# Moving 30 of 2048 score units of an attention kernel from the exponential of ScalarE to a polynomial on VectorE

## The chip, the cores and the metric

The kernel runs on one core of a Trainium2 chip. A core has TensorE (PE, matrix products into PSUM), ScalarE (ACT, functions such as exp), VectorE (DVE, elementwise work), GpSimd (POOL) and SyncE (SP, which here only issues transfers). The engines run their own instruction queues in order and meet through semaphores. The metric is the time of one execution on the device, in microseconds (us); lower is better. Matrix products have a weight load (PEld) ahead of them, which the profile lists for itself.

## What is computed

```python
def reference(A_x, A_wqkv, A_wo, B_x, B_wqkv, B_wo, gate_w):
    x = A_x                                             # (1, 2048, 640), bf16
    g = sigmoid((x * gate_w).sum(-1, keepdims=True))
    a = A_ref(x, A_wqkv, A_wo)    # full attention: 32 heads of 20, softmax over all 2048 keys
    b = B_ref(x, B_wqkv, B_wo)    # local attention: 32 heads of 20, 8 keys at distances 0, 2, ..., 14 back
    return g * a + (1 - g) * b
```

Both branches project x to queries, keys and values with a 640 x 1920 matrix, scale the scores by 20 ** -0.5, and project the result with a 640 x 640 matrix. `B_x` is not used. The exponentials of the full branch are by far the largest piece: 32 heads x 2048 x 2048 of them.

## The kernel before

**Score units.** The full branch is cut into 4 blocks of 512 queries (`qc`), 8 quads of 4 heads (`q`), 16 blocks of 128 keys (`kb`) and 4 heads in a quad (`j`). One (qc, q, kb, j) is a *unit*: a matmul of 128 keys by 512 queries (`mk_qk`, L1107), an exponential from PSUM to an SBUF buffer in bf16 (`mk_exp`, L1122), and a matmul of that with the values (`mk_pv`, L1130), which adds 21 rows (20 values and the sum) to one PSUM bank, `OB`. There are 2048 units. A (qc, q) is a *head group* of 64 units; there are 32, numbered `gi`.

**Steps.** Units are taken in order, alternately three and two at a time (`ST`), in the banks 0 to 2 and 3 to 4. One such set is a step, and one instruction of ScalarE does its exponentials. There are 819 steps. The scores of step s + 2 are issued after the exponential of step s. Value matmuls come in batches, some steps later; six buffers (`ebuf`) hold the exponentials until then.

**Lanes.** All other work is put between the steps by a planner that runs while the program is written. It keeps a model clock for each engine, with a cost for each instruction. Each piece of side work is a Python generator, a *lane*, with a first and a last step (`_Lane`). A lane yields before each piece, and `ready` lets it go on when the model finds room on TensorE (`lim_pe`) or VectorE (`lim_dve`) in the present step. Lanes whose name begins with a letter of `EAGER` have precedence. Others are paced by their window: they are due when they have spent less than their share. `force` writes out a lane without regard to room, where something needs its result at once. The banks 6 and 7 are shared by all lanes through `take` and `give`.

The lanes are: keys, queries and values of the full branch (`gen_k`, `gen_q`, `gen_v`, mostly in head groups 0 to 7, but queries in every group); `gen_norm` for each finished group, which transposes `OB` (`do_norm`, L630), divides by the sums (L638 to L644) and transposes back into a slot of `oTn` (L647), with the scratch tile `rg`; and, for each of the four query blocks `tc`, the local branch: `gen_F` (queries and keys of the local branch, L796, the products of L827 and sums over heads, to eight score rows), `gen_K` (values, L859, the softmax of L877 to L893, and the weighted sum on VectorE, L935 to L951), and `gen_fold` (output projection of both branches together, L677, with one output transfer for each 128 rows). For the last query block `gen_prefold` does most of the fold early (L698, L699), and `last_fold` the rest after the loop.

**Order of the local branch.** `FWIN`, `KWIN` and `OWIN` (L1258 to L1260) give the windows of the lanes F, K and O (fold) for each query block, in head groups; `gstep` turns head groups into steps. K waits for the F of its block; the last addition for each 128 rows of a K, L951, waits until the fold of the block before is through (L948), since both use `oBacc`. `oTn` has `NOT` slots, so that the normalisation of group `NOT` writes the slot of group 0, and the fold of its query block must be done by then (L1365 to L1368).

**Filler.** Where a step leaves TensorE without enough work, `idle_mm` (L1246, L1250) writes matmuls on dead data.

Of the kernel before, what the change touches and what calls it, by code (L numbers as in the profile page):

```python
# [5 lines left out]
FP32 = mybir.dt.float32  # L6
# [18 lines left out]
PADB = (WIN - 1) * DIL  # L25
SCALE = float(DH) ** -0.5
VW = 22


class _Task:  # L30
# [202 lines left out]
def _build(ctx, nc, A_x, A_wqkv, A_wo, B_wqkv, B_wo, gate_w, out):  # L233
# [49 lines left out]
    rg = [sb([P, 512], FP32, "rg")] * 2  # L283
    rr = [sb([P, 16], FP32, "rr%d" % i) for i in range(2)]
    rgn = [sb([P, 16, 32], BF16, "rgn")] * 2
    NOT = 16
    oTn = sb([P, NOT, 512], BF16, "oTn")
    itmp = oTn[:, 13, 0:256].bitcast(I32)
    stmp = oTn[:, 14, 0:320].bitcast(I32).rearrange("p (c k) -> p c k", c=CN)
    stmpf = oTn[:, 15, 0:320].bitcast(FP32).rearrange("p (c k) -> p c k", c=CN)  # L290
    zg = sb([P, KBN], FP32, "zg")
    gA = sb([P, 4 * KBN], FP32, "gA")
    gB = sb([P, KBN], FP32, "gB")
# [123 lines left out]
    free_at = {6: 0.0, 7: 0.0}  # L417
    forcing = [0]
    cur = [None]
    EAGER = "kqv"  # L420

    wanting = set()

# [17 lines left out]
    def give(b, evac):  # L441
        held[b] = False
        if cur[0] is not None:
            cur[0].hold -= 1
        free_at[b] = evac.fin + 56.0

    def after(t):
        return ("t", t.fin + 56.0)
# [96 lines left out]
    def gen_q(gi):  # L545
        qc, q = divmod(gi, NQUAD)
        i = gi % 2
        yield ("dve", 370.0, 0.0)
        yield after(mk_wq(q, i))
        while ("KM", q) not in sch.bufs:  # L550
            yield ("poll",)
        b = yield from take()
        t = yield from chain(b, proj_mms(b, WqP[i], qc), [("WqP", i), "xT"])
        yield ("dw", t.fin, 690.0, 0.0)
        t = q_abs(b, gi)
        while ("KM", q) not in sch.bufs:
            yield ("poll",)
        yield ("t", max(t.fin, sch.bufs[("KM", q)][0].fin))
        yield ("pe", MM, 1.0)
        t = q_km(b, q)  # L560
        yield ("dw", t.fin, 690.0, 0.0)
        give(b, q_cp(b, gi))
# [86 lines left out]

    bdone = {}  # L650
    folddone = {}
    FW = D // 2

    def b_mm(o, blk, c0, dp):
# [11 lines left out]
    def gen_fold(qc):  # L666
        while not bdone.get(qc) or not all(normdone.get(qc * NQUAD + q) for q in range(NQUAD)):
            yield ("poll",)
        for blk in range(4):
            for hf in range(2):  # L670
                c0 = FW * hf
                b = yield from take()
                o = bank[b][:, 0:FW]
                mms = [b_mm(o, blk, c0, dp) for dp in range(CN)] + [a_mm(o, qc, q, blk, c0) for q in range(NQUAD)]
                t = yield from chain(b, mms, b_rd(blk) + a_rd(qc, range(NQUAD)), cost=140.0)
                yield ("dw", t.fin, 490.0, 0.0)
                give(b, T("dve", lambda e, b=b, blk=blk, c0=c0: e.tensor_copy(outsb[:, c0:c0 + FW], bank[b][:, 0:FW]),  # L677
                          reads=[("bk", b)], writes=["outsb"], cost=460))
            T("sp", lambda e, blk=blk: e.dma_start(out_v[:, 4 * qc + blk, :], outsb[:, :]),
              reads=["outsb"], writes=[("outd", qc, blk)], dma=True)  # L680
        folddone[qc] = True

    NPF = NQUAD - 2
# [162 lines left out]
    def gen_K(tc):  # L846
# [80 lines left out]
        for bl in range(4):  # L927
            ai = bl % 2
            for w in range(WIN):
                av = fap(bw, attnT[ai][:, w * P:w * P + 1], [[0, CN], [1, P]])  # L930
                off = PADB - DIL * w + bl * P
                vv = vB4[:, :, off:off + P]
                yield ("dve", 822.0, 822.0)
                if w == 0:
                    T("dve", lambda e, vv=vv, av=av: e.tensor_tensor(blkacc[:, :, :], vv, av, ALU.mult),  # L935
                      reads=[("aT", ai), "vB4"], writes=["blkacc"], cost=822)
                    if bl < 3:
                        yield ("dve", 460.0, 460.0)
                        tr = mk_rep(bl + 1)
                    continue  # L940
                T("dve", lambda e, vv=vv, av=av: e.tensor_tensor(tmpB, vv, av, ALU.mult),  # L941
                  reads=[("aT", ai), "vB4"], writes=["tmpB"], cost=822)
                yield ("dve", 822.0, 822.0)
                if w < WIN - 1:
                    T("dve", lambda e: e.tensor_tensor(blkacc[:, :, :], blkacc[:, :, :], tmpB, ALU.add),  # L945
                      reads=["tmpB"], writes=["blkacc"], cost=822)
                else:
                    while tc >= 1 and not folddone.get(tc - 1):  # L948
                        yield ("poll",)
                    acc = oBacc[:, :, bl * P:(bl + 1) * P]  # L950
                    T("dve", lambda e, acc=acc: e.tensor_tensor(acc, blkacc[:, :, :], tmpB, ALU.add),  # L951
                      reads=["tmpB", "blkacc"], writes=[("oBacc", bl)], cost=822)
                if w == 3 and bl < 3:
                    yield after(tr)
                    b = yield from take()
                    yield ("pe", 550.0, 300.0)
                    tm = mk_aT(bl + 1, b)
                if w == 4 and bl < 3:
                    yield ("dw", tm.fin, 690.0, 690.0)
                    give(b, ev_aT(bl + 1, b))  # L960
        bdone[tc] = True


    mk_wk(0)
# [120 lines left out]
    free_at[6] = free_at[7] = t_  # L1085


    units = [(qc, q, kb, j) for qc in range(QCN) for q in range(NQUAD) for kb in range(KBN) for j in range(4)]
    steps = []
    u = 0  # L1090
    while u < len(units):
# [27 lines left out]
    def mk_exp(s):  # L1119
        b0 = ST[s % 2][0]  # L1120
        n = len(steps[s])
        return T("act", lambda e: e.activation(ebuf[s % NEB][:, 0:512 * n], ps[:, b0 * 512:(b0 + n) * 512], ACTF.Exp, scale=SCALE),  # L1122
                 reads=[("bk", b0 + i) for i in range(n)], writes=[("ebuf", s % NEB)], cost=ED[n])

    def mk_pv(s, us, cost):

        def fn(e):
            ins = None
            for i, (qc, q, kb, j) in us:
                ins = e.matmul(bank[OB][32 * j:32 * j + DH + 1, :], vA[:, q, kb, VW * j:VW * j + DH + 1],  # L1130
                               ebuf[s % NEB][:, i * 512:(i + 1) * 512], start=(kb == 0), stop=(kb == KBN - 1))
            return ins

        rd = {("ebuf", s % NEB)}
        wr, ac = [], []
        for i, (qc, q, kb, j) in us:
            rd.add(("vA", q, kb // 3))
            (wr if kb == 0 else ac).append(("ob", j))
        T("pe", fn, reads=sorted(rd, key=str), writes=wr, accum=ac, cost=cost)

    lanes = []
# [5 lines left out]
    def lane(gen, name, s0, s1, total, pos=None):  # L1147
        g = _Lane(gen, name, s0, s1, total)
        if pos is None:
            lanes.append(g)  # L1150
        else:
            lanes.insert(pos, g)
        return g
# [75 lines left out]

    def gstep(g):  # L1230

        return int(g * KBN * 4 / 2.5)

    def idle_mm():

# [16 lines left out]
              reads=["zt", "ident"], accum=[("ob", j) for j in range(4)], cost=MM)  # L1252
        return True

    kl, vl, ql, foldl = {}, {}, {}, {}
    vl[0] = lane(gen_v(0, 2), "v0", 0, 22, 10)
    lane(gen_late(), "late", 22, gstep(3), 1)
    FWIN = ((3.0, 8.6), (8.6, 13.2), (13.3, 18.3), (18.4, 23.5))  # L1258
    KWIN = ((8.7, 13.0), (13.2, 18.3), (18.4, 23.5), (23.6, 29.2))
    OWIN = ((13.0, 16.5), (18.4, 23.0), (23.6, 28.5))  # L1260
    FTOT, KTOT, OTOT = 58.0, 25 * 250.0 + 5 * 690 + 5 * 300 + 690 + 1880 * 2 + 1215 + 950 + 1500 + 4 * (460 + 690 + 15 * 822), 104.0
    for tc in range(4):
        lane(gen_F(tc), "F%d" % tc, gstep(FWIN[tc][0]), gstep(FWIN[tc][1]), FTOT)
    for tc in range(4):
        lane(gen_K(tc), "K%d" % tc, gstep(KWIN[tc][0]), gstep(KWIN[tc][1]), KTOT)
        if tc < 3:
            foldl[tc] = lane(gen_fold(tc), "O%d" % tc, gstep(OWIN[tc][0]), gstep(OWIN[tc][1]), OTOT)
    pre = lane(gen_prefold(3), "pre", gstep(30) + 4, NS - 3, 88.0)

    def lead(q):  # L1270
# [14 lines left out]
    for s in range(NS):  # L1285
# [4 lines left out]
        if first:  # L1290
            ng = gi + 1
            if ng < QCN * NQUAD:
                nqc, nq_ = divmod(ng, NQUAD)
                g_end = gstep(gi + 1)
                if nqc == 0:
                    if nq_ % 2 == 1 and nq_ < NQUAD - 1:
                        p = (nq_ + 1) // 2
                        vl[p] = lane(gen_v(p), "v%d" % p, s + (20 if s == 0 else 2), gstep(gi + 2) + 8, 16.0)
                    ql[ng] = lane(gen_q(ng), "q%d" % ng, s + 4, g_end - 8 - lead(ng), 6.0, 2 if s == 0 else 1)
                else:  # L1300
                    ql[ng] = lane(gen_q(ng), "q%d" % ng, s + 2, g_end - 10, 6.0, 0)
        E = mk_exp(s)
        odd = s % 2 == 1
        block[0], block[1] = False, 0.0
# [66 lines left out]
                        lane(gen_norm(g1), "norm%d" % g1, s, s + 1, 1.0, 0)  # L1371

        if gend:
            flush(False, True)
        npend = s - pend[0][0] + 1 if pend else 0
        if (odd and npend >= 3) or s >= NS - 2:
# [92 lines left out]
```

## Time and profile before

| what | value |
|---|---|
| median of 3 runs | 962.57 us (961.73 to 962.77) |
| the profiled execution | 961.62 us |
| its span | 959.8 us |
| granted TensorE clock | 0.999 |
| instructions | 16367 |
| matmuls of L1107, L1130, L1246 | 2068, 2048, 316 |
| DMA | 12.86 MB, mean 13 GB/s |

The span runs from the first to the last instruction. Rows of groups read: line, engine, operation, output<-input with shapes, number; then busy time in us and the mean of one in ns; then idle time of the engine just before them. The rows of digits are the busy share in tenths in 40 equal slices of 24 us. Pieces of a chain read: start in us, length in us, what. The first exponential of the loop starts at 19.3 us, the last at 950.5 us.

### The profile page before, as it was taken

What the parts mean: (1) busy time and instruction counts of PE and PEld (TensorE: products, weight loads), DVE (VectorE), ACT (ScalarE), POOL (GpSimd) and SP (SyncE); (2) the same over time, 40 slices, a digit from 0 to 9 for tenths busy, and PEclk for the clock granted to TensorE, in tenths of its full rate; (3) what the DMA queues carried; (4) which work ended last, traced back from release to release, by engine and by line L of the source; (5) the groups of instructions that cost most, each with busy time, mean ns of one, the idle gap of its engine ahead of it and who ended that gap; (6) DMA issues with size and microseconds to landing.
All of it is one profiled execution on the core that took longest, in us unless ns stands there. A gap on an engine that the chain in (4) does not pass through costs nothing.

```text
span 959.8 us, 16367 instructions
## 1 busy us (share of the span) xinstructions
PE 860.9 (90%) x6317; PEld 288.6 (30%) x6418; DVE 572.2 (60%) x1054; ACT 943.2 (98%) x845; POOL 3.1 (0%) x7
## 2 busy tenths in 40 slices
PE   8999898998898888889988889999989998998887
PEld 5333333322222222223322222333222233222232
DVE  5585443445424888762457798355888635897232
ACT  5999999999999999999999999999999999999997
POOL 1000000000000000000000000000000000000000
PEclk9999999999999999999999999999999999999999
DMA  9000000000000000000000000000000000000000
GB/s 312 5 1 22 15 1 1 1 25 12 1 1 1 1 1 1 2 1 8 15 8 1 1 1 1 8 8 8 9 1 1 1 9 14 9 1 1 1 1 29
DMA packets 12032, 12.86 MB, mean 13 GB/s; under 512 B 3380, under 2 KB 11316, under 8 KB 11956
## 3 DMA queue, kind: packets, MB, share of 16 engines
q1 hardware_dynamic: 9844, 11.43, 3.7%
q8 instruction: 53, 0.87, 0.4%
q10 hardware_dynamic: 2112, 0.37, 0.2%
q14 instruction: 23, 0.19, 0.1%
HBM read 9.18 MB, written 2.62 MB: 12 GB/s over the span
## 4 chain that ended last, share of the span: by engine, by line
ACT 73%; issue 17%; PE 8%; DMA 1%; DVE 1%; SPq 0%; ACTq 0%
ACT ebuf L1122 73%; PE ps L1107 3%; PE ps L1246 2%; PE ps L387 1%; PE ps L1130 1%; DMA x_tm<-in_A_x_dram 1%; ACT L_sb L884 0%; PE ps L980 0%; PE ps L719 0%; DVE Kmax L1011 0%; PE ps L811 0%; PE ps L576 0%; PE ps L911 0%; DVE oTn L738 0%; SPq L325 0%
## 5 line engine op out<-in xcount | busy, mean ns | idle before, releaser
L1122 ACT ACTIVATE ebuf<-ps 128x1536 bf16<-128x1536 f32 (+1 forms) x819 | 929.0, 1372 | 1.0
L1107 PE MATMUL ps<-qT,kT 32*128 32x512 bf16 x2068 | 321.9, 382 | 67.0 <-ACT ebuf L1122 54.7
L1107 PEld LDWEIGHTS ps<-qT,kT 32*128 32x128 bf16 x2068 | 89.0, 91 | 347.1 <-issue 145.1
L1130 PE MATMUL ps<-ebuf,vA 128*21 128x512 bf16 x2048 | 172.0, 382 | 0.0
L1246 PE MATMUL ps<-xT,ident 128*128 128x512 bf16 x316 | 122.7, 389 | 16.1 <-PE ps L1107 6.3
L941 DVE TENSOR_TENSOR bw<-vB,bw 128x640 f32<-128x640 bf16 x112 | 91.8, 820 | 2.1
L945 DVE TENSOR_TENSOR blkacc<-blkacc,bw 128x640 f32<-128x640 f32 x96 | 79.0, 823 | 2.9
L827 DVE TENSOR_TENSOR prod<-qk 128x512 bf16<-128x512 bf16 x160 | 57.4, 418 | 20.0 <-PE ps L811 19.8
L630 DVE STREAM_TRANSPOSE rg<-ps 128x512 f32<-128x512 f32 x31 | 22.2, 717 | 78.1 <-PE ps L1130 78.1
L1130 PEld LDWEIGHTS ps<-ebuf,vA 128*21 128x21 bf16 x2048 | 42.0, 90 | 72.2 <-issue 50.4
L1246 PEld LDWEIGHTS ps<-xT,ident 128*128 128x128 bf16 x358 | 34.3, 96 | 97.1 <-PE ps L1246 58.7
L387 PE MATMUL ps<-xT,WqkB 128*128 128x512 bf16 x179 | 58.2, 384 | 2.2 <-PE ps L1107 1.4
L796 DVE CAST qk<-ps 128x512 bf16<-128x512 f32 x40 | 27.5, 687 | 48.0 <-PE ps L387 46.0
L387 PE MATMUL ps<-woA_r,oTn 128*128 128x320 bf16 x240 | 50.4, 302 | 0.1
L387 PE MATMUL ps<-xT,WqP 128*128 128x512 bf16 (+1 forms) x154 | 43.3, 375 | 1.5 <-issue 0.6
L566 DVE CAST qT<-ps 128x512 bf16<-128x512 f32 x31 | 21.4, 690 | 38.4 <-PE ps L387 38.4
L387 PE MATMUL ps<-xT,WkP 128*128 128x512 bf16 (+1 forms) x151 | 42.6, 375 | 1.9 <-issue 1.1
L399 DVE TENSOR_SCALAR kT<-ps,e 128x512 bf16<-128x512 f32 x28 | 21.0, 749 | 36.8 <-PE ps L387 36.6
L583 DVE CAST qT<-ps 128x512 bf16<-128x512 f32 x31 | 21.4, 689 | 22.3 <-PE ps L576 22.1
L387 PE MATMUL ps<-WvA,oBacc 128*128 128x320 bf16 x160 | 33.1, 301 | 0.5 <-PE ps L1107 0.4
L859 DVE CAST vB<-ps 128x512 bf16<-128x512 f32 x20 | 13.7, 686 | 26.9 <-PE ps L387 26.9
L470 PE MATMUL ps<-WvA,xT 128*128 128x160 bf16 (+1 forms) x320 | 29.5, 233 | 0.0
(109 smaller groups left out, 484.2 us busy)
## 6 DMA issues: line engine op xcount, KB each, us to landing
x_tm<-in_A_x_dram SPq DMA_DIRECT2D x3, 640.0 KB
out_dram<-outsb SPq DMA_DIRECT2D x12, 160.0 KB
WqkB<-in_B_wqkv_dram SPq DMA_DIRECT2D x1, 1600.0 KB
WqkA<-in_A_wqkv_dram SPq DMA_DIRECT2D x2, 700.0 KB
qk<-in_B_wqkv_dram SPq DMA_DIRECT2D x1, 800.0 KB
woA_r<-in_A_wo_dram SPq DMA_DIRECT2D x32, 25.0 KB
WvA<-in_B_wo_dram SPq DMA_DIRECT2D x5, 160.0 KB
x_tm<-in_A_x_dram SPq DMA_DIRECT2D x2, 320.0 KB
```

The costliest lines, as they stand in the source:

```text
L387: ins = e.matmul(o, l, r, start=(k0 + k == 0), stop=(k0 + k == n - 1))
L470: ins = e.matmul(bank[b][:, i_ * wn:(i_ + 1) * wn], xT[:, c, kb * P:(kb + 1) * P], WvA[:, c, w0:w0 + wn], start=(c == 0), stop=(c == CN - 1))
L566: T("dve", lambda e: e.tensor_copy(qt[:, :], bank[b]), reads=[("bk", b)], writes=[("qT", gi % NQT)], cost=690)
L630: return T("dve", lambda e: e.transpose(rg[i][:, :], bank[OB]), reads=[("ob", j) for j in range(4)], writes=["rg"], cost=720)
L796: give(b, T("dve", lambda e, dst=dst, b=b: e.tensor_copy(dst, bank[b]), reads=[("bk", b)], writes=[key], cost=690))
L827: t = T("dve", lambda e, r=r, f=f, off=off: e.tensor_tensor(prod[r][:, :], qB[:, f, :], kB[:, f, off:off + 512], ALU.mult), reads=["qB", " ...
L941: T("dve", lambda e, vv=vv, av=av: e.tensor_tensor(tmpB, vv, av, ALU.mult), reads=[("aT", ai), "vB4"], writes=["tmpB"], cost=822)
L945: T("dve", lambda e: e.tensor_tensor(blkacc[:, :, :], blkacc[:, :, :], tmpB, ALU.add), reads=["tmpB"], writes=["blkacc"], cost=822)
L1107: ins = e.matmul(bank[b0 + i], kT[32 * j:32 * j + 32, q, kb * P:(kb + 1) * P], qT[gi % NQT][32 * j:32 * j + 32, :], start=True, stop=True)
L1122: return T("act", lambda e: e.activation(ebuf[s % NEB][:, 0:512 * n], ps[:, b0 * 512:(b0 + n) * 512], ACTF.Exp, scale=SCALE), reads=[("bk" ...
L1130: ins = e.matmul(bank[OB][32 * j:32 * j + DH + 1, :], vA[:, q, kb, VW * j:VW * j + DH + 1], ebuf[s % NEB][:, i * 512:(i + 1) * 512], start ...
L1246: T("pe", lambda e: e.matmul(bank[b], ident[:, :], xT[:, 0, 0:512], start=True, stop=True), reads=["xT", "ident"], writes=[("bk", b)], cos ...
```

## The change

For 30 of the 2048 units the exponential is taken from ScalarE. `XN` says how many units of each of the 32 head groups (0, 1 or 2), `XPOS` which. They are left out of `units`, so the steps are made of the 2018 that remain. Each of the 30 becomes a lane of its own, `gen_x`, with precedence (`EAGER` gets an x), in a window inside its head group. It takes bank 6 or 7, makes the scores there, and computes the exponential with eight instructions of VectorE in fp32: a multiply-add that puts the score, times log2 e, into the exponent field of a floating-point number; the split into exponent and mantissa by bit masks; and a polynomial of the mantissa. Then a value matmul of its own adds to `OB`. What is not done when the group ends is forced ahead of the group's last value matmuls. Two fp32 buffers `xb` are added; `rg` is used as a third, between two normalisations.

The local branch gets other windows, its lanes are listed in another order (K, then folds, then F), and the last addition of a K now waits for the fold of its own 128 rows rather than for the whole fold. `oTn` has 14 slots instead of 16, and `gstep` counts the uneven groups.

```diff
+XC4 = 0.013534167746750096
+XA = (-0.5785127719334512, 30.316837144955663, -17.76242689806009, 576.1803657752102)
+XMUL = SCALE * 1.4426950408889634 * 2.0 ** 23
+XADD = (127.0 + np.log2(XC4)) * 2.0 ** 23
+XN = (0, 0, 1, 1, 1, 2, 2, 0, 1, 0, 0, 0, 0, 1, 2, 0, 0, 1, 1, 1, 1, 1, 0, 1, 2, 2, 1, 2, 1, 2, 1, 2)
+FWIN = ((3.1, 4.4), (7.0, 11.7), (14.3, 18.8), (21.1, 25.7))
+KWIN = ((6.3, 11.3), (6.0, 16.6), (15.3, 22.4), (24.3, 29.9))
+OWIN = ((8.5, 12.7), (15.5, 20.2), (21.7, 25.8))
+XPOS = ((7, 1), (9, 2), (5, 0))
...
-    NOT = 16
+    NOT = 14
+    xb = [sb([P, 512], FP32, "xb%d" % i) for i in range(2)]
...
-    EAGER = "kqv"
+    EAGER = "kqvx"
...
+            foldblk[(qc, blk)] = True
...
-                    while tc >= 1 and not folddone.get(tc - 1):
+                    while tc >= 1 and not foldblk.get((tc - 1, bl)):
...
+    def gen_x(gi, k, u):
+        qc, q, kb, j = u
+        while k > 0 and not xdone.get((gi, k - 1)):
+            yield ("poll",)
+        while gi > 0 and not normdone.get(gi - 1):
+            yield ("poll",)
+        A, B, C = xA[:, :], xB[:, :], xC[:, :]
+        kA, kB_, kC = "xA", "xB", "rg"
+        b = yield from take()
+        yield ("pe", MM, 0.0)
+        t = T("pe", lambda e: e.matmul(bank[b], kT[32 * j:32 * j + 32, q, kb * P:(kb + 1) * P], qT[gi % NQT][32 * j:32 * j + 32, :],
+                                       start=True, stop=True),
+              reads=[("kT", q, kb // 4), ("qT", gi % NQT)], writes=[("bk", b)], cost=MM)
+        yield ("dw", t.fin, 690.0, 690.0)
+        give(b, T("dve", lambda e: e.tensor_scalar(A, bank[b], float(XMUL), float(XADD), op0=ALU.mult, op1=ALU.add),
+                  reads=[("bk", b)], writes=[kA], cost=690))
+        Ai, Bi = A.bitcast(I32), B.bitcast(I32)
+        ops = [
+            (430.0, lambda e: e.tensor_scalar(Ai, A, float(2 ** 23), None, op0=ALU.max), [kA], [kA]),
+            (430.0, lambda e: e.tensor_scalar(Bi, Ai, 0x7FFFFF, 0x3F800000, op0=ALU.bitwise_and, op1=ALU.bitwise_or), [kA], [kB_]),
+            (690.0, lambda e: e.scalar_tensor_tensor(C, B, XA[0], B, ALU.add, ALU.mult), [kB_], [kC]),
+            (430.0, lambda e: e.tensor_scalar(Ai, Ai, 0x7F800000, None, op0=ALU.bitwise_and), [kA], [kA]),
+            (690.0, lambda e: e.scalar_tensor_tensor(B, C, XA[2], B, ALU.add, ALU.add), [kC, kB_], [kB_]),
+            (690.0, lambda e: e.scalar_tensor_tensor(C, C, XA[1], B, ALU.add, ALU.mult), [kB_, kC], [kC]),
+            (690.0, lambda e: e.scalar_tensor_tensor(xe, C, XA[3], A, ALU.add, ALU.mult), [kA, kC], [kB_]),
+        ]
+        for c, fn, rd, w in ops:
+            yield ("dve", c, c)
+            t = T("dve", fn, reads=rd, writes=w, cost=c)
+        while (gi, j) not in obstart or (q, kb // 3) not in vdone:
+            yield ("poll",)
+        yield after(t)
+        yield ("pe", MM, 0.0)
+        T("pe", lambda e: e.matmul(bank[OB][32 * j:32 * j + DH + 1, :], vA[:, q, kb, VW * j:VW * j + DH + 1], xe, start=False,
+                                   stop=False, skip_group_check=True),
+          reads=[kB_, ("vA", q, kb // 3)], accum=[("ob", j)], cost=MM)
+        xdone[(gi, k)] = True
...
-    FWIN = ((3.0, 8.6), (8.6, 13.2), (13.3, 18.3), (18.4, 23.5))
-    KWIN = ((8.7, 13.0), (13.2, 18.3), (18.4, 23.5), (23.6, 29.2))
-    OWIN = ((13.0, 16.5), (18.4, 23.0), (23.6, 28.5))
...
+            n = len(xunits[gi])
+            for k in range(n):
+                sa, sb_ = s + 6, gstep(gi + 1) - 6
+                xl[(gi, k)] = lane(gen_x(gi, k, xunits[gi][k]), "x%d.%d" % (gi, k), sa + k * (sb_ - sa) // n,
+                                   sa + (k + 1) * (sb_ - sa) // n, 4740.0, 0)
...
         if gend:
+            for k in range(len(xunits[gi])):
+                if not xdone.get((gi, k)):
+                    late.append((s, "x", gi, k))
+                    force(xl[(gi, k)], s)
             flush(False, True)
```

## The prediction

> **What bounds the kernel now.** I read the page's engine rows first, then the waits of ScalarE, then ScalarE's groups with shapes kept apart, then the chain of waits in a quiet stretch, then a table of stretches as long as a head group (64 units, 29.15 us).
>
> Engine rows and waits: is one engine full, and does it ever wait for another?
>
> ```profile
> PE 860.9 (90%) x6317; PEld 288.6 (30%) x6418; DVE 572.2 (60%) x1054; ACT 943.2 (98%) x845; POOL 3.1 (0%) x7
> DVE  5585443445424888762457798355888635897232
> ACT  5999999999999999999999999999999999999997
> ```
> ```profile
> ACT xT L990 <- PE ps L980: 4.6, 4, 2.1
> ACT WvB L752 <- PE ps L745: 3.1, 2, 2.8
> ```
>
> The longest waits of ScalarE (ACT) lie before its main loop (L990) and after it (L752). Inside it no wait is listed. VectorE (DVE) is 60% busy, unevenly.
>
> ```profile
> L1122 ACT ACTIVATE ebuf<-ps 128x1536 bf16<-128x1536 f32 x410 | 650.4, 1586 | 0.6
> L1122 ACT ACTIVATE ebuf<-ps 128x1024 bf16<-128x1024 f32 x409 | 473.4, 1158 | 0.3
> ```
>
> 819 steps, alternately of 3 and 2 units, make the loop. Consecutive steps overlap, so a mean duration is not a pace. The pace is read from the chain, where the two-unit steps start again and again:
>
> ```profile
> 609.67 0.86 ACT ebuf L1122
> ...
> 614.18 0.87 ACT ebuf L1122
> ...
> 618.70 0.87 ACT ebuf L1122
> ...
> 623.22 0.87 ACT ebuf L1122
> ```
>
> 609.67 to 623.22 is six pairs of steps: 13.55 us, 2.26 us a pair, 0.452 us a unit. First and last step start at 19.3 and 950.5 us, so 409 pairs take 931.2 us, where 409 x 2.26 is 924.3. Of the 6.9 us over, some 3.7 are the four exponentials of the local branch (L884, 1.19 us each, 0.93 after overlap with their neighbours). About 3.2 us are stalls. The loop is as good as solid ScalarE.
>
> Does it stay so when VectorE is busy?
>
> ```profile
> 544.00:573.10 29.10, 25.01 (x185) 7.79 (x188) 26.42 (x42) 29.10 (x27) 0.00 (x0) 1.00 0.00 1
> 573.10:602.30 29.20, 26.81 (x177) 8.13 (x180) 22.46 (x34) 29.12 (x27) 0.00 (x0) 1.00 0.00 1
> 602.30:631.40 29.10, 28.52 (x207) 9.84 (x210) 9.37 (x18) 29.10 (x27) 0.00 (x0) 1.00 0.02 6
> ```
>
> The columns are window, length, busy time of PE, PEld, DVE, ACT, POOL, granted clock, DMA. VectorE goes from 26.42 us (91%) to 9.37 us (32%); ScalarE is solid in both. So VectorE work as such does not slow ScalarE.
>
> **Part 1, removed from ScalarE.** The counts in the diff add up to 30 units, so 2018 are left, exactly 404 steps of three and 403 of two: 807 steps, 12 fewer, six of each kind. 6 x 2.26 = 13.56 us on the path that sets the end. Nothing before the loop or after it changes in kind.
>
> **Part 2, added to VectorE.** A unit is eight instructions of 128x512, each dependent on one before it. The first reads PSUM: L566 gives 0.690, L399 0.749; I take 0.69. Four are scalar_tensor_tensor, not in the trace: nearest are tensor_tensor in fp32, 0.490 for 320 elements (L644) and 0.823 for 640 (L945); between them 512 gives 0.69. Three are tensor_scalar on 32-bit data in SBUF. Their bounds are 0.293 (L567, 512 elements of 16 bits) and 0.69 (as the PSUM read). The nearest rows are L602 (fp32 from int32, 160 elements, 0.229) and L526 (16 elements, 0.176); their slope, 0.37 ns an element, gives 0.36 at 512, which I take. Dependent neighbours stand apart by about 0.034, as here:
>
> ```profile
> 953.19 0.20 DVE L731 RECIPROCAL rr<-rg 128x8 f32<-128x8 f32 x1
> 953.43 0.17 DVE L732 TENSOR_TENSOR rr<-rr,gA 128x8 f32<-128x8 f32 x1
> ```
>
> Sum: 0.69 + 3 x 0.36 + 4 x 0.69 + 8 x 0.034 = 4.8 us; ends 4.6 and 5.8. Thirty are 144 us (138 to 175). DVE busy should come to about 572 + 30 x 4.53 = 708 us of a span near 948, 75%. All of it lies beside ScalarE as long as VectorE keeps up.
>
> The Trainium skill (VectorE: DVE Perf Modes, "The perf-mode tier table") gives an fp32 tensor_scalar in SBUF two elements a cycle, 1227 ns for 2048 elements. An estimate from that page is 0.43 us at 512, a unit of 5.0 us and thirty of 150. No row of the trace has this operation at this size.
>
> The Trainium skill also speaks against the change: ScalarE: Activation LUTs, "Rules for kernel authors", says to use ScalarE for exp since it is the only option. By the rule there would be nothing to move, and the gain would be zero. The trace agrees on the price (0.45 us on ScalarE against some 5 on VectorE), but it also shows 388 us of idle VectorE, and the diff builds the exponential from a bit trick and a polynomial.
>
> **Part 3, does VectorE keep up?** Per head group the always present work (query projection and normalisation, L369, L566, L567, L583, L630 to L647) is 4.4 us. A local chunk is 65.8 us of value and attention work ("K": rows L935 to L951, 197.0, and L859 to L918, 66, over four) and 22.7 us of logits ("F": L796, L827, L837 over four). The tightest stretch is groups 24 to 31: 33 fixed, 65.8 for K3, 8 for the rest of F3, 3.9 for a fold, 7.8 for the pre-fold, 13 units x 4.8 = 62: 181 us of about 226, 80%. The table shows 91% in one group's length, and 82% over the three from 514.8 to 602.3 (22.87 + 26.42 + 22.46 of 87.5). So it should fit, with little over. Groups 6 to 12 hold 34 fixed, K0, F1, some 20 of F0 and three units, 157 of 203 us; there an overrun only pushes later local work.
>
> **Part 4, TensorE.** Each unit adds a lone score matmul and a lone value matmul, about 0.22 us each when pipelined, and two changes of weights of about 0.1: 0.64 us, 19 us in all. L1246 and L1250 are 339 filler matmuls on dead data, some 73 us at 0.216, written only where TensorE has nothing else; they are the cover. Without it ScalarE would lose up to 19 us.
>
> **Part 5, the new waits.** The value matmul waits for the eight-step chain. TensorE runs in order, so the next scores, and then ScalarE, queue behind it. The planner holds it back until its model has the chain finished, and forces it at the end of the group. The bound below is 0.8 us: the loop now has about 233 bank hand-overs to VectorE and 3.2 us of stalls, 0.014 each, and 60 new ones come. The bound above is 6 us: each unit disturbs one pair by 0.2 us. I take 2.0, nearer the lower, since the quiet and the busy stretch alike show no loss.
>
> **Part 6, at nothing.** Fourteen slots for normalised groups instead of 16: group 14 now needs fold 0, which follows K0 (window to 11.3 groups), so 3.7 groups, 107 us, cover a fold of 104 matmuls at 0.14 (four of L745 take 0.72 us, one 0.30), about 15 us. Without that cover TensorE would run those 15 us with no scores and eat the gain. Waiting per block instead of per chunk only relaxes. The output transfers that move with the folds stand alone in SP's queue after the weights. The scratch tile shared with normalisation stays on one engine.
>
> Sum: 961.62 (profiled execution; 959.8 of span and 1.8 around it) - 13.56 + 2.0 = 950.1. The median of the runs, 962.57, is 0.95 above that execution, so I predict **951.0 us**; with the bounds of part 5, 949.8 to 955.
>
> **Rivals.** (a) *VectorE overfull in groups 24 to 31* (chance 0.16): the dear end of part 2 makes it 194 of 226, 86%, which no stretch of three groups has shown; K3 and with it the pre-fold slip until they are forced ahead of the tail, unhidden. At 6 us of lost time the result is 957; a slip that eats the gain would be 962. For it: the last row of digits that is heavy now (slices 34 and 35, 8 and 9) is where 13 units go. Against it: the pre-fold waits 3.9 us between pieces now and can be pressed together. (b) *Late chains stop TensorE* (slower, 0.13): if a unit is not through when its group ends, it is forced, and TensorE stands for what is left of the chain, up to 4.8 us, less the one step of scores that ScalarE has in hand, 1.1: 3.7 us a time. From four such units of 30, or 0.45 us a unit on average, the gain is gone; eight give 961.6 - 13.6 + 8 x 3.7 = 978. For it: VectorE also serves keys and values in groups 2 to 6, where seven units lie, and at 48.5 to 77.6 it is at 22.7 us already. Against it: the units have precedence, and each has 13 steps or more, 14 us, for 4.8 us. (c) *The gain is paid back exactly* (within 0.2%, 0.05): a 2.26 us pair that becomes 2.29 by contention for PSUM or SBUF, 404 x 0.03 = 12 us, 961. The stretches above speak against it.
>
> **Chances.** Forecast 0.66 (948.5 to 954), (a) 0.16 (954 to 960.6), (c) 0.05, (b) 0.13. Faster by over 0.2%, about what a measurement of this kernel can tell from no change, is 0.82; within it 0.05; slower 0.13. The range leaves out (b), (c) and the worst of (a): 948.5 (nothing lost, less half a microsecond between runs) to 958.5.
>
> **What would show it.** Right: 404 and 403 rows of the two shapes at L1122's successor; a pair still 2.26 us; ScalarE without a wait in the loop; DVE about 708 us; tensor_scalar near 0.36 and scalar_tensor_tensor near 0.69; fewer fillers. Wrong: TensorE waiting on VectorE before the lone value matmul; ScalarE idle at the ends of groups with units; the pre-fold ending after the last exponential; a tail longer than the 8 us from 952 now.

## The result and the profile after

The changed kernel takes 949.95 us (median of 4 runs, 948.64 to 952.39), the kernel before 962.56: a ratio of 0.9874, 95% interval 0.985 to 0.9897. The prediction was 951.0, range 948.5 to 958.5.

The page of the changed kernel's profiled execution (951.03 us), engine rows and digits, to set beside those of before:

```profile
span 949.2 us, 16591 instructions
PE 867.3 (91%) x6359; PEld 285.5 (30%) x6359; DVE 699.9 (74%) x1294; ACT 930.3 (98%) x833; POOL 3.1 (0%) x7
DVE  5486665775688878668788876688898578898735
ACT  5999999999999999999999999999999999999997
```

VectorE went from 572.2 to 699.9 us and its row is flatter; ScalarE's row is what it was. The changed kernel was run again beside the experiments, and that profile (948.54 us) is the better one for an account, since its clock was full through the whole loop. Its ScalarE groups with shapes apart, then ScalarE's waits:

```profile
L1187 ACT ACTIVATE ebuf<-ps 128x1536 bf16<-128x1536 f32 x404 | 637.0, 1577 | 0.4
L1187 ACT ACTIVATE ebuf<-ps 128x1024 bf16<-128x1024 f32 x403 | 463.3, 1150 | 0.8 <-ACT ebuf L1187 0.2
```
```profile
ACT xT L1049 <- PE ps L1039: 4.5, 4, 1.9
ACT WvB L767 <- PE ps L760: 3.1, 2, 2.8
...
ACT ebuf L1187 <- ACT ebuf L1187: 0.2, 1, 0.2
```

404 and 403 steps, as counted, and still nothing of weight in the loop that ScalarE waits for. From the first exponential of the loop (L1187) to the last step it is 918.25 us, where before it was 931.13: 12.9 us less, where six pairs are 13.56. The 0.7 us between is the net of what the 30 units and the new order of the local branch cost in stalls. Span 959.8 to 946.7 is 13.1; prologue and tail stayed.

What one unit is on VectorE, from the groups of VectorE of the same profile:

```profile
L998 DVE TENSOR_SCALAR xb<-ps 128x512 f32<-128x512 f32 x30 | 20.6, 688 | 14.7 <-PE ps L994 11.0 <-PE ps L1172 3.6
L1002 DVE TENSOR_SCALAR xb<-xb 128x512 int32<-128x512 f32 x30 | 12.8, 426 | 1.0
L1004 DVE SCALAR_TENSOR_TENSOR rg<-xb 128x512 f32<-128x512 f32 x30 | 20.7, 689 | 0.7
```

And who waited for the end of a chain, from the list of waits:

```profile
PEld ps L1017 <- DVE xb L1008: 1.0, 2, 0.7
PE ps L1017 <- DVE xb L1008: 0.4, 1, 0.4
```

Of 30 lone value matmuls (L1017) one waited for its chain, 0.4 us (its weight load, 0.7). It is the last unit of group 14, which the planner had to force, and no wait of ScalarE follows it.

A chain that nothing interrupts lasts 4.72 us from the first start to the last end (the shortest here, and the median of e_force below is 4.73); half of the 30 took more than 6.5 us here, since other work of VectorE went in between.

### The profile page after: what moved, and what is told of

Read it like the earlier page. It is cut to its first block, busy times and chain, and to the rows that moved or that the text cites. A ratio compares the mean times of both kernels' runs of the same rounds, so it can differ in the third digit from the quotient of the medians.

```text
span 949.2 us, 16591 instructions
## 1 busy us (share of the span) xinstructions
PE 867.3 (91%) x6359; PEld 285.5 (30%) x6359; DVE 699.9 (74%) x1294; ACT 930.3 (98%) x833; POOL 3.1 (0%) x7
## 4 chain that ended last, share of the span: by engine, by line
ACT 68%; issue 16%; PE 15%; DVE 1%; DMA 1%; SPq 0%; ACTq 0%; DVEq 0%
ACT ebuf L1187 67%; PE ps L1172 5%; PE ps L400 4%; PE ps L1314 2%; PE ps L1195 2%; DMA x_tm<-in_A_x_dram 1%; PE ps L1039 1%; PE ps L483 0%; ACT L_sb L899 0%; PE ps L994 0%; DVE Kmax L1070 0%; PE ps L926 0%; PE ps L886 0%; PE ps L826 0%; PE ps L1017 0%
## 5 line engine op out<-in xcount | busy, mean ns | idle before, releaser
L1187 ACT ACTIVATE ebuf<-ps 128x1536 bf16<-128x1536 f32 (+1 forms) x807 | 915.6, 1358 | 2.2 <-PE ps L1172 1.0
L1172 PE MATMUL ps<-qT,kT 32*128 32x512 bf16 x2048 | 318.6, 382 | 66.0 <-ACT ebuf L1187 56.7
L1314 PE MATMUL ps<-xT,ident 128*128 128x512 bf16 x272 | 105.5, 388 | 6.7
L400 PE MATMUL ps<-xT,WqkB 128*128 128x512 bf16 x200 | 63.5, 385 | 0.0
L400 PE MATMUL ps<-woA_r,oTn 128*128 128x320 bf16 x240 | 48.5, 302 | 0.0
L1314 PEld LDWEIGHTS ps<-xT,ident 128*128 128x128 bf16 x272 | 26.0, 96 | 71.8 <-PE ps L1314 46.1
L400 PE MATMUL ps<-xT,WqP 128*128 128x512 bf16 (+1 forms) x165 | 47.2, 384 | 0.1
L400 PE MATMUL ps<-xT,WkP 128*128 128x512 bf16 (+1 forms) x165 | 46.1, 381 | 0.0
L400 PE MATMUL ps<-xT,WvB 128*128 128x512 bf16 x100 | 31.7, 384 | 0.0
L998 DVE TENSOR_SCALAR xb<-ps 128x512 f32<-128x512 f32 x30 | 20.7, 688 | 14.7 <-PE ps L994 9.9
L596 DVE CAST qT<-ps 128x512 bf16<-128x512 f32 x31 | 21.3, 688 | 13.2 <-PE ps L589 13.1
```

The source lines that it names most:

```text
L400: ins = e.matmul(o, l, r, start=(k0 + k == 0), stop=(k0 + k == n - 1))
L596: return T("dve", lambda e: e.tensor_copy(qT[gi % NQT][:, :], bank[b]), reads=[("bk", b)], writes=[("qT", gi % NQT)], cost=690)
L1172: ins = e.matmul(bank[b0 + i], kT[32 * j:32 * j + 32, q, kb * P:(kb + 1) * P], qT[gi % NQT][32 * j:32 * j + 32, :], start=True, stop=True)
L1314: T("pe", lambda e: e.matmul(bank[b], ident[:, :], xT[:, 0, 0:512], start=True, stop=True), reads=["xT", "ident"], writes=[("bk", b)], cos ...
```

## Experiments

### Is the gain the twelve steps? (no unit moved; only the first eleven)

```diff
-XN = (0, 0, 1, 1, 1, 2, 2, 0, 1, ...)
+XN = (0,) * 32                                                          # e_nox
+XN = (0, 0, 1, 1, 1, 2, 2, 0, 1, 0, 0, 0, 0, 1, 2, 0) + (0,) * 16       # e_first
```

> The changed kernel with no unit moved: the new windows of the local branch, the new order of lanes, the wait per block and 14 slots stay, but ScalarE does all 2048 units in 819 steps. Theory (the whole gain is the 12 steps that ScalarE no longer has, at 2.26 us a pair): 962.6 us, between 961.5 and 963.5. Rival (the new windows bring part of it by taking stalls away): below 961, at the most by the 3.2 us of stalls that the loop of before had, so down to 959.3.

Measured: 963.75 us (10 runs, 961.48 to 966.81), ratio 1.0014 (1.0002 to 1.0027). The new windows, order and slots alone gain nothing; they cost about 1 us at the median, a little more than either side had expected, and none of the ten runs had a clock of 1.0 (0.999 to 0.992). Its profile (963.88 us, clock 0.998) has a span 2.2 us longer than before. Of these, 1.2 us lie ahead of the loop, where the clock is half until 10.4 us (before: until 6.3), and 1.1 us in it. A stretch of 3.4 us at half clock at 317.6 us alone makes the loop 1.8 us longer, with this wait of ScalarE, which the kernel before does not have:

```profile
ACT ebuf L1187 <- PE ps L1172: 1.2, 2, 0.8
```

> Only the 11 units of the head groups 1 to 16 (numbers 0 to 15) are moved: 2037 units in 815 steps, four fewer than before. Theory (the gain is the steps, at 1.13 us each, and no fixed cost comes with the change): 4.5 us less than the run with no unit moved at the same clock, 957 to 959. Rival (the chains cost something each, hidden by something else in the whole change): above 959.5.

Measured: 961.04 us (10 runs), ratio 0.9992 (0.9977 to 1.0007). The median lies on the rival's side. The runs spread from 958.06 to 964.67, and with the clock: the four at 0.998 or 0.999 took 958.06, 959.01, 959.03 and 960.84, two at 0.995 and 0.996 took 961.24 and 960.85, and the four at 0.992 or 0.993 took 962.58 and 964.42 to 964.67. The profiled one (964.67 us, 0.992) has two stretches of 6.8 us at half clock, at 282 and 487 us, and the pairs of steps there are some 5.5 us longer than in the profile of 948.54 us; without that it would have been about 959, the upper end of the theory's span. The median is 2.7 us below that of e_nox (on another chip), where four steps are 4.5, so this run alone does not exclude a cost of the units. The whole change leaves little room for one: run beside e_nox (950.66), it lies 13.1 us below it, of 13.56. The gain of a small dose can be lost to the clock.

### Does a later chain stop TensorE? (one instruction doubled, the planner not told)

```diff
             t = T("dve", fn, reads=rd, writes=w, cost=c)
+            for _ in range(1 if c == 690.0 and rd == [kB_] else 0):
+                kept = (dict(clk), t.fin)
+                t = T("dve", fn, reads=rd, writes=w, cost=c)
+                t.fin = kept[1]
+                clk.update(kept[0])
```

> In each of the 30 units one scalar_tensor_tensor is done twice, which the planner is not told: the plan is the same, but each chain on VectorE ends 0.72 us later (0.689 and 0.034), 21.7 us more in all. Theory (VectorE has room, and TensorE's queue can take a late value matmul because ScalarE has scores in hand): at most 0.1 us a unit, 949 to 952. Rival (b) of the prediction (TensorE stands behind the late chain and ScalarE behind it): nearly all of it, 30 x 0.6 = 18 us, 967.

Measured: 955.93 us (955.04 to 956.74), ratio 0.9933 (0.9918 to 0.9948). Between the two: 5.3 us over the same kernel without the doubling (950.66), 0.18 us a unit of the 0.72 added. Between runs of like clock (0.998 and 0.996) it is 4 to 5 us. ScalarE's waits of this profile:

```profile
ACT ebuf L1192 <- PE ps L1177: 5.0, 9, 1.3
```

Nine waits, 5.0 us, where the undisturbed profile of the changed kernel has none on TensorE. Four lone value matmuls stand for their chain (0.35 to 1.2 us), and ScalarE waits after three of them; three more waits follow TensorE work held up behind VectorE in other ways. Rival (b) is a real mechanism; with the chain at its true length it has just enough slack not to act. The other three waits, 2.0 of the 5.0 us, stand in a stretch of 6.8 us at half clock at 489 us. That stretch makes 2.3 of the 6.7 us by which this loop is longer than the undisturbed one, so the clock has a share in this price.

### What does a forced chain cost? (units opened only at the end of their group)

```diff
-                sa, sb_ = s + 6, gstep(gi + 1) - 6
+                sa, sb_ = gstep(gi + 1) - 2, gstep(gi + 1)
```

> The lanes of the 30 units open only two steps before their group ends, so that all 30 are forced there; the rest of the kernel is planned anew around it. Rival (b) of the prediction, at its own price: TensorE stands for the chain of 4.8 us less the one step of scores that ScalarE has in hand, 3.7 us a unit, 949 + 111 = 1060 us. Theory of slack (ScalarE has two steps in hand, 2.26 us): 2.5 us a unit, 1025. If forced chains are free, as the two that the planner forced in the changed kernel (groups 5 and 14) seem to be: 950.

Measured: 1163.78 us (1161.66 and 1165.89), ratio 1.2089 (1.2022 to 1.2156): 7.2 us a unit, about twice the price in the prediction. ScalarE's waits, then ScalarE in order of time at the end of group 2, then stretches there (window, length, PE, PEld, DVE, ACT, POOL, granted clock, DMA):

```profile
ACT ebuf L1187 <- PE ps L1172: 206.2, 96, 23.1
```
```profile
113.19 2.37 ACT L1187 ACTIVATE ebuf<-ps 128x1024 bf16<-128x1024 f32 x2 [3.84 <-PE ps L1172]
115.92 1.02 ACT L1187 ACTIVATE ebuf<-ps 128x1024 bf16<-128x1024 f32 x1 [0.36 <-PE ps L1172]
117.85 1.45 ACT L1187 ACTIVATE ebuf<-ps 128x1536 bf16<-128x1536 f32 x1 [0.91 <-PE ps L1172]
```
```profile
108.00:112.00 4.00, 0.48 (x7) 0.12 (x7) 3.36 (x6) 1.35 (x2) 0.00 (x0) 0.91 0.08 19
112.00:116.00 4.00, 3.15 (x22) 0.58 (x19) 3.16 (x8) 2.45 (x3) 0.00 (x0) 0.50 0.06 13
```

The stand itself is 3.84 us, the 3.7 of rival (b); in the 14 groups with one unit it lies between 2.0 and 6.0 us, but for one of 12.0. But TensorE, idle for 3.5 of 4 us, then runs at half clock for 10 us, and ScalarE waits again and again; the pairs of steps after this stand are 2.8 us too long in all. In the eight groups with two units the stand was 10 to 23 us.

### What do windows and slots do? (old windows with and without the units)

```diff
-FWIN, KWIN, OWIN, the order of lanes and the wait per block of the changed kernel
+those of the kernel before                                        # e_oldwin
+those of the kernel before, and XN = (0,) * 32                    # e_nox_oldwin
```

> The kernel before, in its own windows and order, with 14 slots for normalised groups instead of 16 and no unit moved. The prediction costed 14 slots at nothing while a fold has 107 us of cover, and at 15 us without it. Here the fold's window (13.0 to 16.5 groups) runs past the end of group 14, so it is forced there: theory: 962.6 plus the part of the 15 us that is not yet done, 966 to 977, with the wait of ScalarE near 445 us. Rival (forced work hides behind the scores in hand): 962.6.

Measured: 980.27 us, ratio 1.0183 (1.0148 to 1.0219). The wait, from ScalarE in order of time, then rows of the forced fold inside it:

```profile
474.98 15.92 ACT L1187 ACTIVATE ebuf<-ps 128x1536 bf16<-128x1536 f32 x14 [15.67 <-PE ps L1172]
```
```profile
465.00 0.49 DVE L691 CAST outsb<-ps 128x320 bf16<-128x320 f32 x1 [4.20 <-DMA out_dram<-outsb]
465.64 1.40 PE L400 MATMUL ps<-WvA,oBacc 128*128 128x320 bf16 x5 [2.77 <-DVE outsb L691]
466.83 2.34 PE L400 MATMUL ps<-woA_r,oTn 128*128 128x320 bf16 x8
```

One wait of 15.67 us, at 459 us, the end of group 14. That it equals the 15 us of the prediction is chance: the 15 us were for all 104 matmuls of a fold, and here 39 had been issued before (from 422.9 us on). The 65 left took 0.24 us each and not 0.14. They come in five pieces of 13, and after the first each piece waits for the output copy of the one before (L691); one copy waited 4.2 us for an output transfer, and one piece ran at half clock. Other stands, at stretches of less than full clock, add some 2 us. 14 slots are free only with an earlier fold.

In the changed kernel the fold has little to spare. Its last output copy, then the first step of the normalisation of group 14, which needs the slot (profile of 948.54 us):

```profile
449.38 0.48 DVE L691 CAST outsb<-ps 128x320 bf16<-128x320 f32 x1
454.10 0.72 DVE L643 STREAM_TRANSPOSE rg<-ps 128x512 f32<-128x512 f32 x1 [0.80 <-PE ps L1195]
```

The prediction counted on 107 us between the end of K0 and this point. There were 67, and the fold was through after 63 of them.

> The 30 units in the windows, the order of lanes and the wait of the kernel before; the 14 slots stay. Theory (VectorE alone decides, and it has room in any order): 950. Rival (the windows are what lets the units be hidden: with the old ones the fold of the first query block is forced at the end of group 14, 15 us of TensorE without scores, and K3 and the pre-fold are forced ahead of the tail): 965 or more, with ScalarE waiting near 440 us and near 930 us.

Measured: 1016.76 us, ratio 1.0562 (1.0519 to 1.0605). ScalarE's two great waits, in order of time:

```profile
482.10 18.27 ACT L1187 ACTIVATE ebuf<-ps 128x1536 bf16<-128x1536 f32 x16 [25.44 <-PE ps L1172]
...
1005.89 2.37 ACT L1187 ACTIVATE ebuf<-ps 128x1024 bf16<-128x1024 f32 x2 [37.60 <-PE ps L1172]
```

The first is the fold, forced as without the units, longer here: 94 of its 104 matmuls were still to do, and from 470 to 480 us the clock is at 0.57. The second is new: K3 and the pre-fold stand ahead of the tail, from 970 to 990 us with VectorE busy for 19.3 of 20 us and TensorE for 2.6. VectorE's total is 701.2 us here, as in the changed kernel: the sum fits, the order does not. Windows, order of lanes and the wait per block were changed together; which of them counts most is not shown.

### Is there room for more? (six units more)

```diff
-XN = (0, 0, 1, 1, 1, 2, 2, 0, 1, 0, 0, 0, 0, 1, 2, 0, 0, 1, ...)
+XN = (0, 0, 1, 1, 1, 2, 2, 1, 1, 0, 1, 1, 1, 1, 2, 1, 1, 1, ...)
```

> Six units more, one each in the groups 7, 10, 11, 12, 15 and 16: 36 in all, 805 steps. Theory (VectorE, 74% busy, has room for more): two steps fewer, 2.3 us less, about 947. Rival (the room is used up where a deadline stands: K0 ends later by some 20 us, and the fold of the first query block is forced at the end of group 14 and that of the second at the end of group 22): 2.3 us less and up to 15 us more for each forced fold, 955 to 975, with ScalarE waiting near 440 and 670 us.

Measured: 1000.83 us, ratio 1.0397 (1.0355 to 1.0439), dearer than both. In order of time, ScalarE:

```profile
468.42 10.49 ACT L1187 ACTIVATE ebuf<-ps 128x1536 bf16<-128x1536 f32 x9 [14.94 <-PE ps L1172]
...
989.94 1.94 ACT L1187 ACTIVATE ebuf<-ps 128x1024 bf16<-128x1024 f32 x2 [34.18 <-PE ps L1172]
```

The first is the forced fold, where expected, with 52 of its matmuls still to do. The second fold cost nothing like 15 us; the surprise is 34 us at the end. No unit was added after group 16, yet K3 and the pre-fold come too late: each K waits for the one before it, so the delay is passed on through all four. Their last additions (L966) start at 413, 624, 836 and 975 us, in the changed kernel at 386, 558, 730 and 888.

### Where does the spread between runs come from?

The four runs of the changed kernel lay at 948.64 and 948.87 with a mean granted clock of 1.0, and at 951.03 and 952.39 with 0.996. In the profile of 951.03 (stretches, columns as above):

```profile
282.00:284.00 2.00, 1.38 (x13) 0.36 (x12) 2.00 (x2) 2.00 (x3) 0.00 (x0) 1.00 0.00 0
284.00:286.00 2.00, 2.00 (x9) 0.54 (x6) 1.05 (x2) 1.87 (x2) 0.00 (x0) 0.51 0.00 0
286.00:288.00 2.00, 2.00 (x9) 0.34 (x7) 0.88 (x2) 1.11 (x2) 0.00 (x0) 0.64 0.04 8
```

TensorE has little to do at the end of a group (no filler is written once the value matmuls are flushed), here with an exponential of the local branch on top; then its clock is half for 3.4 us and ScalarE waits 1.0 us.

```diff
+    HOOK = {227: 4, 228: 1, 229: 2}          # e_fill: steps after the local exponential, fillers each
...
+        for _ in range(HOOK.get(s, 0)):
+            kept = (dict(clk), list(block))
+            if idle_mm():
+                sch.lists["pe"][-1].fin = kept[0]["pe"]
+            clk.update(kept[0])
+            block[:] = kept[1]
...
     pro_tr(0)
+    T("pe", pe_keep, reads=["ident", "rgn"], writes=[("bk", 7)])    # e_warm: 4 matmuls of L365's kind
     pro_tr(1)
```

e_both has both edits. e_clk has the prologue's four and `HOOK = {227: 3, 229: 1, 401: 1, 403: 1, 503: 3, 505: 1}`, and does the scores of the steps 205, 407 and 460 two, two and one times more.

> The changed kernel as it stands, beside the runs below on the same chip. Four runs of it gave 948.64, 948.87, 951.03 and 952.39 us, the two lower ones at a mean granted clock of 1.0, the two higher ones at 0.996. Theory (the spread is TensorE's clock: it is halved for 3.4 us at a time where TensorE has stood too long, at 7.4 us and at 284 us in the profile of 951.03): the runs again fall near 948.7 with a clock of 1.0 and near 951 to 952 with less, and the profile shows the stretch at 284 us at half clock whenever its time is above 950. Rival (noise of another kind): times and clocks do not go together.

Measured: 948.54, 950.03, 951.30 and 952.34 us at clocks of 1.0, 0.998, 0.996 and 0.996; ratio 0.9884 (0.9868 to 0.9901). Time and clock go together, some 1.4 to 1.9 us for 0.002. The one run profiled was that at 1.0 and has no half clock at 284 us.

> Seven filler matmuls on dead data more, in the three steps after the first exponential of the local branch (278.8 us in the profile), where TensorE stood still before its clock was halved at 284 us; the plan is otherwise the same, instruction for instruction. Theory (too little work on TensorE there halves the clock): the clock stays 1.0 from 270 to 300 us, ScalarE has no wait there (it had 0.74 and 0.28 us), and the time of runs that were above 950 falls by 1.2 us, so a median near 949 and a spread of under 2 us. Rival (the halving comes from elsewhere, or the wait from VectorE): half clock and the two waits stay, median as the run without it.

Measured: 950.69 us (949.88, 949.93, 951.45, 951.73), ratio 0.9879 (0.9865 to 0.9894). The median did not move, two runs stayed at 0.996. The profile (949.88) is at full clock there, but so is one without the filler. Not settled by this run. The fillers have a price: in this profile they make the loop 0.4 us longer, and ScalarE waits 0.3 us there.

> The changed kernel with four filler matmuls on dead data in the prologue, after the transposes of the first piece of x, where TensorE stands for the second piece: 0.96 us in the profile that took 948.54 us, 1.79 us in the one that took 951.03, where the clock was then halved from 7.4 to 10.9 us and the loop began 1.1 us later. Theory (that stand halves the clock): full clock from some 5 us on in the profile, the loop's first exponential near 19.3 us, and a median lower by about half a microsecond to one, 949.5 to 950.2, since some of the runs lose it now. Rival (the pieces of x arrive late by themselves): clock and time as without the filler, median 950.7.

Measured: 951.60 us (948.67 to 953.79 at clocks of 1.0 to 0.993), ratio 0.9887 (0.9871 to 0.9903). In the profile the clock was full from 7.2 us on and the loop began at 19.6 us, but the loop had half clock twice, for 6.8 us each at 253 and 488 us, and the median is no better. As an improvement it failed.

> The four fillers in the prologue and the seven after the first exponential of the local branch together. Theory (spread between runs is half clock after a stand of TensorE, and these two places are the ones that matter): all runs near 948.6 at a clock of 1.0. Rival (it comes in other places as well, as in e_fill, two of whose runs stayed at 0.996): spread of over 1.5 us and a median of 949.5 to 950.7.

Measured: 949.36 us (949.17, 949.33, 949.38, 951.86), ratio 0.9875 (0.9859 to 0.989). Three runs at 1.0, one at 0.996: nearer to the theory, not clear of the rival.

> The changed kernel with small filler at every place where TensorE is busy for less than some 70% of 3.4 us: four matmuls in the prologue, ten on dead data at the ends of the head groups near 279 and 594 us, and score matmuls done again (two, two and one times) near 251, 482 and 542 us, where no bank is free for dead data. The plan is otherwise the same. In the profiles of the runs before, half clock came at 253, 284 and 489 us, each time just after such a place, and a time goes up by some 1.2 us for each 0.002 of mean clock. Theory (these stands of TensorE make the spread): all runs at a clock of 0.999 or more and within 1 us of 949, so below both the kernel before and the median of the changed kernel, 950.7. Rival (the halving is not bound to these places): again runs at 0.996 and a spread of over 2 us, median 950 to 951.

Measured: 949.22 us (949.08, 949.20, 949.24, 950.72), all at a clock of 1.0; ratio 0.9864 (0.9847 to 0.988). Of the two stretches that went wrong elsewhere, e_warm first (half clock in the second), then e_clk:

```profile
478.00:485.00 7.00, 5.99 (x50) 2.05 (x50) 5.03 (x8) 7.00 (x7) 0.00 (x0) 1.00 0.01 4
488.00:495.00 7.00, 6.94 (x32) 1.40 (x32) 3.50 (x8) 4.86 (x5) 0.00 (x0) 0.53 0.00 1
```
```profile
478.00:485.00 7.00, 6.36 (x51) 2.05 (x47) 5.06 (x7) 7.00 (x7) 0.00 (x0) 1.00 0.01 4
488.00:495.00 7.00, 6.55 (x48) 1.79 (x46) 5.90 (x10) 7.00 (x8) 0.00 (x0) 1.00 0.00 0
```

Of all variants this is the lowest ratio and the narrowest in clock. It is clear of the kernel before; its interval overlaps that of the changed kernel (0.9868 to 0.9901), so that it beats that one is likely, not shown. Its run of 950.72 us, also at full clock, has a loop as short as the one of 948.54 us; there the tail after the last exponential was 1.8 us longer.

## Why the prediction was right

**Part 1** held to the step: 807 steps, 13.56 us of them, 12.9 seen in the loop, and the gain is gone without the units (e_nox).

**Part 2**: the scalar_tensor_tensor took 0.683 to 0.689 (taken 0.69), the read from PSUM 0.688 (0.69). The tensor_scalar in SBUF took 0.418 to 0.426, and 0.36 from the slope of two short rows was too low. The unit of 4.8 came out through two errors that cancel. The tensor_scalars are 0.06 dearer each, but the chain is not as serial as assumed: the steps at L1005 and L1006 do not need the one before them and start some 0.08 us before its end, so that an undisturbed chain lasts 4.72 us (e_force). For the same reason VectorE's busy time rose less than the durations: 30 units are 140.6 us in durations, but where an instruction of another lane follows, the two overlap by some 0.08 us, and busy time rose by 127.7 us, 4.26 a unit. The total is 700, not 708. The estimate of 0.43 us from the page VectorE: DVE Perf Modes ("The perf-mode tier table" of the Trainium skill) was the better one; this trace now shows it. The dear end, 5.8 us a unit, would not have been harmless: e_dup1 lengthens the chains by 0.72 of that 1.0 us and gives back 5.3 us.

The other page weighed there, ScalarE: Activation LUTs ("Rules for kernel authors" of the Trainium skill), has ScalarE as the only option for exp. The runs show another option, at 4.3 us of VectorE for 0.45 us of ScalarE.

**Part 3**: groups 24 to 31 were put at 181 us; from 716 us to 948 us VectorE was busy for 171.7 us, 74%. (The fixed work is a little off in both sums: at 4.4 us a group it is 35 us for eight groups, not 33, and 31 for seven, not 34.) It fitted, but for a reason that the part only touched. A sum per stretch says too little: e_oldwin has the same sum and loses 67 us, e_x36 adds six units where the sum has room and loses 51. What decides is when the chain of folds and K reaches its deadlines.

**Part 4** was not tested by itself; filler fell from 339 to 312 (272 of L1314, 40 of L1318), as it should.

**Part 5** took 2.0 us of stalls; the undisturbed profile has 0.7, just under the lower bound of 0.8. This term was over-sized, since it took every hand-over as equally likely to be late, while in this plan one chain of 30 was. That the first profile, 951.03 us, lies 0.9 above the 950.1 of the sum has another reason, half clock, which no part held: 1.3 us in the prologue (the loop starts at 20.5 us there) and 1.2 in the loop. So the mechanism was right, but the closeness of 951.0 to the median of 949.95 is partly luck: with 0.7 for 2.0 the sum gives 948.8, which is what the runs at full clock took (948.54 to 948.87), and the clock then adds to the other runs what the stalls did not.

**Part 6**: nothing was lost, as said, but the cover was 67 us, not 107, and 4 us of it were left. The price without cover was too low: e_nox_oldwin paid 15.67 us for 65 of the 104 matmuls, e_oldwin 25.4 for 94. The 0.14 us of a matmul leave out the output copies and transfers between the pieces.

**Rivals.** (a) did not happen, and its price was too low by far: forced K3 and pre-fold cost 34 and 38 us where they occur, not 6 to 14. (b) did not happen; its stand was sized rightly for one unit (3.84 against 3.7), its whole was not (7.2), for want of the half clock that follows and of the longer stands where a group has two units. (c): a pair is still 2.26 us.

## What to carry to other kernels

When one engine is solid, price what is taken from it at its pace in the chain (here 2.26 us for two steps), and then ask of the engine that takes it over not whether the sum fits, but which deadlines its queue must meet; with the same sum this change gains 13 us in one order and loses 54 in another. Give such work precedence and true costs in the plan: a chain 0.7 us longer than planned gave back nearly half the gain, part of it by the clock. And look at the granted clock of each run before reading differences of 2 us.

## What the hardware showed unexpectedly

TensorE's granted clock fell to half for 3.4 us, or a multiple of it, inside a loop in which TensorE hardly ever stood for longer than 1 us at a time. Within each profile all changes of the clock in the loop lie on one grid of 3.41 us: in e_warm, for example, there are 6.83, 228.69 and 6.83 us between them, 2, 67 and 2 times 3.413. Where the grid lies differs from one execution to the next.

Adding up the matmul rows of the traces window by window on this grid shows what came first. In the window right ahead of each such stretch TensorE was busy for 57% (the changed kernel, at 284 us), 69% (e_nox, 318), 69% (e_dup1, 489), 71 and 59% (e_warm, 253 and 488), 61 and 59% (e_first, 282 and 487), with no single gap over 0.96 us. The lowest windows of the same profiles, and of those without such a stretch, that kept their clock have 63% (the kernel before, 477), 64% (e_dup1, 281 and 455) and 67% (the profile of 948.54 us, 279 and 480). In e_clk, where none of the runs lost it, the lowest window anywhere in the loop has 76%. So a low share comes ahead of the loss, but between 63 and 71% it went both ways, and no threshold follows.

The grid gives a reason why two runs of one kernel differ. The dip near 280 us is the same in both profiles of the changed kernel: 55% over its worst 3.41 us. In the one of 951.03 us a window of the grid lies on it (280.6 to 284.0 us, 57%), and the clock is lost; in the one of 948.54 us the grid cuts it in two (67% at the lowest), and it is kept. That this decides the spread of all runs is not shown, since only the mean clock of the others is on record.

A stretch of 3.4 us made the loop 1.2 to 1.8 us longer (the changed kernel, e_nox), one of 6.8 us 2.3 to 2.9 (e_warm, e_dup1, e_first). This accounts for the waits of ScalarE on TensorE in the loops of these profiles, but for six of e_dup1.

The Trainium skill (TensorE: Matmul & The Clock Gate, "Why this matters for your kernels") asks for no idle gaps of more than about 3 us between bursts. By that rule this loop would be safe. Here half clock came without any gap of even 1 us ahead of it.
